# A joint image-text attention block: the image probabilities are transposed by ScalarE's DMA queue instead of TensorE

## The chip, the cores and the metric

The kernel runs on one core of one Trainium2 chip. The metric is the time of one execution in microseconds of device time, as a median of several runs. The engines are named as in the profile: PE is TensorE (PEld its weight loads), DVE is VectorE, ACT is ScalarE, POOL is GpSimd, SP is SyncE. A name with a q behind it (SPq, ACTq) is that engine issuing a DMA.

## The reference

Two streams, image (2 batches of 256 tokens) and text (2 batches of 32 tokens), each 1152 wide, in bfloat16. Each stream is layer-normed and modulated by rows computed from `c`; the two are joined for one softmax attention of 288 tokens per batch, projected back separately, gated and added to the input.

```python
hi = _layernorm(x_img) * (1 + sci) + shi          # 2 x 256 x 1152
ht = _layernorm(x_txt) * (1 + sct) + sht          # 2 x 32 x 1152
qkvi, qkvt = hi @ wqkv_img, ht @ wqkv_txt
q, k, v = concat of text and image parts          # 2 x 288 x 1152
p = softmax(q @ k^T * D ** -0.5)                  # 2 x 288 x 288
a = p @ v
out_i = x_img + gai * (a[:, 32:] @ wo_img)
out_t = x_txt + gat * (a[:, :32] @ wo_txt)
```

## The kernel before

The order of the work on every engine is the order in which the kernel's text issues it (`manual_schedule`); waits between engines are put in by the framework. Eleven weight matrices of 2.65 MB (1152 x 1152) stream in on SP's queue in the order of their use, through a ring of five buffers and two fixed homes. The stages on PE, one after another: the modulation scale and the image values (`v_wide`, L255), the image queries and keys (`qk_img`, L512), rows of the text modulation (L402, L406), the text queries and keys (`qk_txt`, L580), then the stage that the change is in, then the output projection (`out_chunk`, L845).

The stage of the change, in its order before:

1. `scores_img` (L613): for each of four blocks (batch b, block q of 128 query tokens) PE computes 128 x 288 scores by nine products; DVE takes the row maximum (L597), ACT the exponential with its row sum (L600, tile `e`), DVE the reciprocal and the scaled probabilities `pb` (L604, L605: 128 x 288, bfloat16), and POOL copies the text columns of `pb` into `px` (L607).
2. `scores_txt_and_gate`: PE makes the text scores (L626, both batches in one tile of 64 rows) and rows of the image gate (L630, L635). ACT copies a first piece of the gate rows to SBUF (L638, `g_sb`), and POOL stores it to a scratch in DRAM by two DMAs (L640). Then comes `softmax_txt` (ACT L669) and the next gate piece (ACT L642). PE makes the text values (L688) and the rest of gate and values (L646, L651, L654). `softmax_txt_norm` gives `pb_tt` (DVE L675), whose text columns POOL copies into `px_t` (L676). The end of the stage takes the text values (DVE L657), the last gate piece (ACT L658, POOL L660) and the last block of values (ACT L661) out.
3. `p_transposes`: for each half kj of the 256 image keys, PE transposes the five 128 x 128 blocks (four image, one text) into one PSUM tile `pk` (L697, ten products against the identity), and DVE (kj = 0) or ACT (kj = 1) copies each batch's 288 columns to `pTs[b]` (L704). Three more transposes make `pX` from the `px` tiles (L707), for the products against the text values.
4. `attn_out`: sums of the values by the transposed probabilities, in three groups of output blocks (L753), with DVE and ACT taking the results out (L766, L768). `full_ops` gives the order inside a group: kj outside, batch inside, so that the first eight products need both batches' first halves.

Behind it POOL reads the gate rows back from DRAM, broadcast over 128 partitions (L803, `gb`), and multiplies a third of the output weights by them (L829, `w_og`); DVE multiplies and adds each output chunk (L851, L852).

A DMA signals its end on one of eight semaphores in rotation, and a DMA that takes a semaphore again waits for the DMA that had it before.

Of the kernel before, what the change touches and what calls it, by code (L numbers as in the profile page):

```python
# [14 lines left out]
def kernel(  # L15
# [14 lines left out]
    nc = tc.nc  # L30
    bf = mybir.dt.bfloat16
    f32 = mybir.dt.float32
    PSUM = bass.MemoryType.PSUM

    B, NI, D = x_img.shape
    NT = x_txt.shape[1]
    P = 128
    KT = D // P
    NTOK = NI + NT
    NIT = (B * NI) // P  # L40
    TPB = NI // P
    NTT = B * NT
    CH = 384
    NCH = D // CH
    VC = 288
# [12 lines left out]
    ps_mm = ctx.enter_context(tc.tile_pool(name="ps_mm", bufs=7, space=PSUM))  # L58
# [11 lines left out]
    def w_view(src):  # L70
        return src.rearrange("(kt p) n -> p kt n", p=P)

    def load_w(src, c0, ksplits=((0, KT),), home=None):
        t = wpool.tile([P, KT, D], bf, tag="w", name="t") if home is None else act.tile([P, KT, D], bf, tag=home, name="w_home")
        for (k0, k1) in ksplits:
            nc.sync.dma_start(t[:, k0:k1, :], w_view(src)[:, k0:k1, c0:c0 + D])
        return t
# [35 lines left out]
    K3 = ((0, 3), (3, 6), (6, KT))  # L113
    K2 = ((0, 5), (5, KT))
# [4 lines left out]
    ident = const.tile([P, P], bf)  # L119
# [64 lines left out]
    v_t = act.tile([P, VW], bf)  # L184
    v_t8 = act.tile([NTT, P], bf)
# [193 lines left out]
    pbs = {}  # L379
# [3 lines left out]
    pxs = [act.tile([P, 2, B, NT], bf, name=f"px_{q}") for q in range(TPB)] + [act.tile([P, 2, B, NT], bf, name="px_t")]  # L383
# [38 lines left out]
    def cols_out(dst, cps, add):  # L422
        nc.vector.tensor_scalar_add(dst, cps[:].rearrange("p (k b) -> p k b", b=B), add)
# [14 lines left out]
    v_wide_out(3, 1)  # L438
    evac(v_i[:, :, NM:D], vacc["n"][:])

    w_k_i = load_w(wqkv_img, D, K3)
    w_sh_t = load_w(wmod_txt, 0)
    w_sc_t = load_w(wmod_txt, D, K2)
    nc.sync.dma_start(x_t[0:P:P // NTT, :], xt_flat[:, :])
    w_q_t = load_w(wqkv_txt, 0, K2)
    w_k_t = load_w(wqkv_txt, D, K2)
    w_ga_i = load_w(wmod_img, 2 * D, K2, home="V")
    w_v_t = load_w(wqkv_txt, 2 * D, K3)
# [4 lines left out]
    gsc = tc.dram_tile([B, D], bf, name="mod_scratch")  # L453
# [136 lines left out]
    qk_txt(w_k_t, 1)  # L590


    qpos = [[0, P, 2 * P], [NT, NT + P, 0]]

    def softmax_img(sps, key):
        nmx = small.tile([P, 1], f32, tag="nmx")
# [6 lines left out]
    def softmax_norm(key, e, rs):  # L603
        nc.vector.reciprocal(rs[:], rs[:])  # L604
        nc.vector.tensor_scalar_mul(pbs[key][:], e[:], rs[:])  # L605
        b, q = key
        nc.gpsimd.tensor_copy(pxs[q][:, :, b, :], pbs[key][:, NI:NTOK].unsqueeze(1).to_broadcast([P, 2, NT]))  # L607

    def scores_img(b, qi):
        q0 = qi * P  # L610
        sps = ps_mm.tile([P, NTOK], f32, tag="mm")
        for ft in range(KT):
            nc.tensor.matmul(sps[:], lhsT=qkTs[0][:, ft, b, q0:q0 + P], rhs=qkTs[1][:, ft, b, :],  # L613
                             start=(ft == 0), stop=(ft == KT - 1))
        return softmax_img(sps, (b, qi))

    CW = 544
    GW = VC + P
    GR = (D - 2 * GW) // NGG

    def scores_txt_and_gate():
        sps = ps_mm.tile([P, NTOK], f32, tag="mm")
        gps = ps_mm.tile([P, GW + GR], f32, tag="mm")
        for ft in range(KT):
            for b in range(B):
                nc.tensor.matmul(sps[NT * b:NT * (b + 1), :], lhsT=qkTs[0][:, ft, b, NI:NTOK], rhs=qkTs[1][:, ft, b, :],  # L626
                                 start=(ft == 0), stop=(ft == KT - 1), tile_position=(0, NT * b))
            for g in range(2):
                r = 64 + 32 * g
                nc.tensor.matmul(gps[r:r + 32, 0:VC], lhsT=sT32[:, ft, :], rhs=w_ga_i[:, ft, g * GW:g * GW + VC],  # L630
                                 start=(ft == 0), stop=(ft == KT - 1), tile_position=(0, r))
        for kt in range(KT):
            for g in range(NGG):
                c0 = 2 * GW + g * GR
                nc.tensor.matmul(gps[32 * g:32 * g + 32, GW:GW + GR], lhsT=sT32[:, kt, :], rhs=w_ga_i[:, kt, c0:c0 + GR],  # L635
                                 start=(kt == 0), stop=(kt == KT - 1), tile_position=(0, 32 * g))
        g_sb = work.tile([P, CW], bf, tag="garow2", bufs=1)
        nc.scalar.copy(g_sb[:, GW:GW + GR], gps[:, GW:GW + GR])  # L638
        for b in range(B):
            nc.gpsimd.dma_start(gsc[b, 2 * GW:D].rearrange("(g j) -> g j", g=NGG), g_sb[b:P:32, GW:GW + GR])  # L640
        st = softmax_txt(sps)
        nc.scalar.copy(g_sb[64:P, 0:VC], gps[64:P, 0:VC])  # L642
        vps = v_txt_wide()
        for kt in range(KT):
            for b in range(B):
                nc.tensor.matmul(gps[NT * b:NT * (b + 1), VC:GW], lhsT=hT_t[:, kt, NT * b:NT * (b + 1)],  # L646
                                 rhs=w_v_t[:, kt, NM:D], start=(kt == 0), stop=False,
                                 tile_position=(0, NT * b))
            for g in range(2):
                r = 64 + 32 * g  # L650
                nc.tensor.matmul(gps[r:r + 32, VC:GW], lhsT=sT32[:, kt, :], rhs=w_ga_i[:, kt, g * GW + VC:(g + 1) * GW],  # L651
                                 start=(kt == 0), stop=(kt == KT - 1), tile_position=(0, r))
        for b in range(B):
            nc.tensor.matmul(gps[NT * b:NT * (b + 1), VC:GW], lhsT=selS[:, b, :], rhs=svn[:],  # L654
                             start=False, stop=True, tile_position=(0, NT * b))
        softmax_txt_norm(*st)
        nc.vector.tensor_sub(v_t[:], vps[:], v_t[:])  # L657
        nc.scalar.copy(g_sb[64:P, VC:GW], gps[64:P, VC:GW])  # L658
        for b in range(B):
            nc.gpsimd.dma_start(gsc[b, 0:2 * GW].rearrange("(g j) -> g j", g=2), g_sb[64 + b:P:32, 0:GW])  # L660
        nc.scalar.copy(v_t8[:], gps[0:NTT, VC:GW])  # L661

    def softmax_txt(sps):
        q = NTT
        nmx = small.tile([P, 1], f32, tag="nmx")
        nc.vector.reduce_max(nmx[0:q, :], sps[0:q, :], axis=AX.X, negate=True)
        e = work.tile([P, NTOK], f32, tag="of", bufs=1, name="e")
        rs = small.tile([P, 1], f32, tag="rst", bufs=1)
        nc.scalar.activation(e[0:q, :], sps[0:q, :], ACT.Exp, bias=nmx[0:q, :], scale=1.0, accum_out=rs[0:q, :])  # L669
        return e, rs  # L670
# [8 lines left out]
    pTs = [work.tile([P, 2, NTOK], bf, tag="pT", name=f"pT{b}") for b in range(B)]  # L679
# [10 lines left out]
                                     start=(kt == 0), stop=(kt == KT - 1), tile_position=(0, r))  # L690
        return ps

    def p_transposes():
        pt = pbs["t"]
        def wide(pk, kj, srcs):
            for src, q0 in srcs:
                nc.tensor.transpose(pk[:, q0:q0 + P], src[:, kj * P:(kj + 1) * P], ident[:])  # L697

        for kj in range(TPB):
            pk = ps_mm.tile([P, B * NTOK], bf, tag="mm", name="pk")  # L700
            wide(pk, kj, [(pbs[(0, 0)], 0), (pbs[(0, 1)], P), (pt, NI),
                          (pbs[(1, 0)], NTOK + NT), (pbs[(1, 1)], NTOK + NT + P)])
            for b in range(B):
                (nc.scalar.copy if kj else nc.vector.tensor_copy)(pTs[b][:, kj, :], pk[:, b * NTOK:(b + 1) * NTOK])  # L704
        pX_ps = ps_mm.tile([P, 2 * NT + NI], bf, tag="mm", name="pX_ps")
        for px, x0 in ((pxs[TPB], 0), (pxs[0], 2 * NT), (pxs[1], 2 * NT + P)):
            nc.tensor.transpose(pX_ps[:, x0:x0 + P], px[:].rearrange("p g b t -> p (g b t)"), ident[:])  # L707
        svp = ps_sm.tile([P, NCOL + B], f32, tag="sm", name="svp")
        select_cols(strips["svr"], svp)
        nc.vector.tensor_copy(pX[:, 0:NTOK], pX_ps[:, NT:NT + NTOK])  # L710
        nc.vector.tensor_copy(pX[:, NTOK:NTOK + NT], pX_ps[:, 0:NT])
        cols_out(sv, svp, 0.0)
# [16 lines left out]
        return {(dt, b): [(acc_bank(), 0, 0, NTOK)] for dts_ in dts for b in range(B) for dt in dts_}  # L729

    def full_ops(dts, acc):
        return [(dt, b, kj, pc) for kj in range(TPB) for b in range(B) for dt in dts for pc in acc[dt, b]]

    def text_ops(dts, acc):
        return [[(dt, b, None, acc[dt, b][n]) for b in range(B)] for dt in dts for n in range(len(acc[dt, B - 1]))]
# [37 lines left out]
    def attn_out():  # L773
# [15 lines left out]
        run(fC + flat(tC), fC + flat(tC))  # L789
        acc_evac(accC, [(dt, b) for b in range(B) for dt in GC])  # L790

    s00 = scores_img(0, 0)
    s01 = scores_img(0, 1)
    softmax_norm(*s00)
    s10 = scores_img(1, 0)
    softmax_norm(*s01)
    s11 = scores_img(1, 1)
    softmax_norm(*s10)
    softmax_norm(*s11)
    scores_txt_and_gate()  # L800
    gb = act.tile([P, B, D], bf, tag="Bt")
    for b in range(B):
        nc.gpsimd.dma_start(gb[:, b, :], gsc[b, :].partition_broadcast(P))  # L803
    xt_q = xt_flat.rearrange("(q h) (g j) -> g q h j", h=2, g=NGG)
    for g in range(NGG):
        nc.gpsimd.dma_start(xf[32 * g:32 * g + 32, :, :], xt_q[g])
    p_transposes()
    aT = act.tile([P, KT, B * NTOK], bf, tag="Q")
    attn_out()

# [112 lines left out]
```

## Time and profile before

| | |
|---|---|
| median of 3 runs | 114.87 us (114.75 to 115.28) |
| the profiled execution | 115.62 us, of which its span 113.8 us |
| PE busy | 109.1 us, 96% of the span |
| DVE, ACT, POOL busy | 76.0, 37.4, 27.6 us |
| SP's DMA queue | 39.05 MB, 89.8% of the 16 DMA engines' span |
| ACT's DMA queue | 0.77 MB, 2.2% |
| TensorE clock granted | 0.998 |

The chain of waits follows the work that ended last back to its start. A line of it gives start, length and what; `x10` means ten instructions. In the timeline a line gives start, busy time, engine, line, operation, `out<-in` with shapes, and in brackets the idle time before it with what ended it. A DMA issue line gives what is moved, from which queue, how often, the size of one and the median time from issue to landing.

### The profile page before, as it was taken

The page shows a single profiled execution, that of the slowest core. Times are in us where ns is not written, and L with a number is a line of the kernel's source. Part 1 is how long each engine was busy: PE and PEld are TensorE (multiplying, and loading weights), DVE is VectorE, ACT ScalarE, POOL GpSimd, SP SyncE. Part 2 cuts the span into 40 slices and gives each one's busy share as a digit, 9 for nine tenths or more (in the row PEclk, how much of TensorE's full clock was granted, in tenths as well). Part 3 has the DMA queues.
Part 4 walks back from the last instruction along what each step waited for, and adds up shares of the span by engine and source line. Part 5 has one row for each costly group of instructions (what it writes and reads, how often), then busy time and mean ns, then how long its engine had stood idle before and what let it go on. Part 6 is the DMA issues. An engine that isn't in the chain of part 4 may idle for free.

```text
span 113.8 us, 2918 instructions
## 1 busy us (share of the span) xinstructions
PE 109.1 (96%) x1227; PEld 65.0 (57%) x1227; DVE 76.0 (67%) x151; ACT 37.4 (33%) x86; POOL 27.6 (24%) x60
## 2 busy tenths in 40 slices
PE   5999997999999999999999999999999999999990
PEld 1356663655644444444446659787687565667670
DVE  1699330756299999999999860236666802998771
ACT  4627500272290062640008934015546700001000
POOL 7000120640050000000000050601450460699300
PEclk9999999999999999999999999999999999999999
DMA  3999999999999999999999999999999999983052
GB/s 84 327 352 344 375 374 408 410 410 413 405 411 407 411 413 405 410 411 412 412 409 412 413 403 406 407 396 377 407 411 404 409 412 407 378 328 132 12 178 69
DMA packets 22839, 40.87 MB, mean 359 GB/s; under 512 B 1375, under 2 KB 6635, under 8 KB 22827
## 3 DMA queue, kind: packets, MB, share of 16 engines
q1 hardware_dynamic: 21547, 39.05, 89.8%
q10 hardware_dynamic: 672, 0.77, 2.2%
q0 software_dynamic: 608, 0.88, 2.1%
q8 instruction: 9, 0.15, 0.5%
q14 instruction: 3, 0.02, 0.1%
HBM read 39.36 MB, written 1.34 MB: 358 GB/s over the span
## 4 chain that ended last, share of the span: by engine, by line
PE 80%; SPq 8%; DMA 8%; issue 1%; DVE 0%
PE qkps L512 31%; PE ps L845 16%; DMA w_sc_i<-in_wmod_img_dram 8%; PE va L255 7%; SPq L98 6%; PE aps L753 5%; PE ps L580 4%; PE sps L613 4%; PE gps L402 3%; PE ops L863 2%; PE ps L688 2%; SPq L94 1%; PE van L267 1%; PE gps L818 1%; PE sps L626 1%; PE mps L217 1%
## 5 line engine op out<-in xcount | busy, mean ns | idle before, releaser
L512 PE MATMUL qkps<-hT_i,t 128*128 128x512 bf16 x162 | 35.6, 379 | 0.0
L512 PEld LDWEIGHTS <-t 128*128 128x128 bf16 x162 | 15.6, 98 | 18.6 <-issue 0.2
L474 DVE SCALAR_TENSOR_TENSOR sacc<-w_v_i,mod_img,sacc 128x1152 f32<-128x1152 bf16 x16 | 22.7, 1419 | 0.5
L255 PE MATMUL va<-w_v_i,hT_i 128*128 128x512 bf16 x72 | 17.5, 380 | 0.0
L845 PE MATMUL ps<-t,aT 128*128 128x384 bf16 x99 | 16.4, 326 | 0.0
L845 PEld LDWEIGHTS <-aT 128*128 128x128 bf16 x117 | 11.0, 98 | 6.9 <-issue 0.5
L851 DVE TENSOR_TENSOR tmp<-ps,gb 128x384 bf16<-128x384 f32 x11 | 6.1, 550 | 6.1 <-DMA gb<-mod_scratch 5.0
L829 POOL TENSOR_TENSOR w_og<-t,gb 128x384 bf16<-128x384 bf16 x9 | 8.7, 1004 | 4.6 <-DMA gb<-mod_scratch 4.6
L255 PEld LDWEIGHTS <-hT_i 128*128 128x128 bf16 x72 | 6.3, 98 | 5.6 <-ACT hT_i L201 0.4
L533 POOL TENSOR_SCALAR svn<-svr 128x128 bf16<-128x128 bf16 x1 | 0.3, 299 | 33.0 <-ACT svr L154 33.0
L140 PE MATMUL wps<-wz 128*128 128x512 bf16 x15 | 6.5, 613 | 1.2 <-DVE wz L125 1.2
L166 DVE BATCH_NORM_STATS2 stats<-x_i 128x6 f32<-128x384 bf16 x12 | 5.8, 541 | 2.5 <-DMA x_i<-in_x_img_dram 2.5
L462 ACT ACTIVATE qT<-qkps 128x512 bf16<-128x512 f32 x9 | 4.7, 602 | 7.1 <-PE qkps L512 7.1
L478 ACT CAST shi<-sacc 128x1152 bf16<-128x1152 f32 x2 | 2.3, 1152 | 13.0 <-DVE sacc L474 13.0
L240 POOL TENSOR_SCALAR hT_i<-hT_i,mod_img 128x128 bf16<-128x128 bf16 (+1 forms) x5 | 2.1, 435 | 15.8 <-DVE mod_img L225 15.8
L766 DVE TENSOR_SCALAR aT<-aps,sv 128x288 bf16<-128x288 f32 (+2 forms) x11 | 4.3, 456 | 2.0 <-PE aps L753 2.0
L235 DVE TENSOR_SCALAR hT_i<-hT_i,mod_img 128x256 bf16<-128x256 bf16 (+1 forms) x16 | 4.3, 328 | 1.7 <-ACT hT_i L212 1.5
L580 PEld LDWEIGHTS <-t 128*128 128x128 bf16 x162 | 5.0, 98 | 0.5
L154 DVE CAST kT<-qkps 128x512 bf16<-128x512 f32 x3 | 2.1, 686 | 4.7 <-PE qkps L512 4.7
L580 PE MATMUL ps<-hT_t,t 128*128 128x64 bf16 x162 | 5.1, 193 | 0.0
L852 DVE TENSOR_TENSOR o<-tmp,x_i 128x384 bf16<-128x384 bf16 x11 | 4.7, 426 | 0.4
L753 PE MATMUL aps<-pT,v_i 128*128 128x288 bf16 (+2 forms) x44 | 4.8, 265 | 0.0
(167 smaller groups left out, 146.2 us busy)
## 6 DMA issues: line engine op xcount, KB each, us to landing
t<-in_wqkv_img_dram SPq DMA_DIRECT2D x6, 864.0 KB, 13.0
t<-in_wmod_txt_dram SPq DMA_DIRECT2D x2, 2592.0 KB, 17.6
t<-in_wqkv_txt_dram SPq DMA_DIRECT2D x2, 1440.0 KB, 14.2
t<-in_wmod_img_dram SPq DMA_DIRECT2D x3, 864.0 KB, 12.3
t<-in_wqkv_txt_dram SPq DMA_DIRECT2D x3, 864.0 KB, 14.2
t<-in_wo_txt_dram SPq DMA_DIRECT2D x3, 864.0 KB, 15.5
t<-in_wqkv_txt_dram SPq DMA_DIRECT2D x2, 1152.0 KB, 15.0
w_v_i<-in_wqkv_img_dram SPq DMA_DIRECT2D x7, 288.0 KB, 7.1
```

Of the source, the lines that this page charges most:

```text
L98: nc.sync.dma_start(w_v_i[:, kt:kt + 1, :], w_view(wqkv_img)[:, kt:kt + 1, 2 * D:3 * D])
L140: nc.tensor.matmul(ps[:], lhsT=wz[:, 0:P], rhs=wz[:], start=True, stop=True)
L166: nc.vector.bn_stats(stats[0:np_, k, :], x_ap[:, k * CH:(k + 1) * CH])
L255: nc.tensor.matmul(ps[:], lhsT=hT_i[:, kt, i * P:(i + 1) * P], rhs=w_v_i[:, kt, half * VW:(half + 1) * VW], start=(kt == 0), stop=(kt == K ...
L462: nc.scalar.mul(out_ap, in_ap, SCALE)
L474: nc.vector.scalar_tensor_tensor(saccs[b][:], w_v_i[:, kt, :], ap, saccs[b][:], op0=ALU.mult, op1=ALU.add)
L512: nc.tensor.matmul(pss[j - j0][:], lhsT=wq[:, kt, j * P:(j + 1) * P], rhs=hT_i[:, kt, :], start=(kt == 0), stop=(kt == KT - 1))
L580: nc.tensor.matmul(ps[:, j - j0, :], lhsT=wq[:, kt, j * P:(j + 1) * P], rhs=hT_t[:, kt, :], start=(kt == 0), stop=(kt == KT - 1))
L753: nc.tensor.matmul(bank[:, off:off + c1 - c0], lhsT=lhsT, rhs=rhs, start=(first[id(bank)] == n), stop=(final[id(bank)] == n))
L829: nc.gpsimd.tensor_mul(w_og[:, dt, 0:CH], w_o_i[:, dt, NG0:D], gb[:, B - 1, NG0:D])
L845: nc.tensor.matmul(ps[:, 0:cw], lhsT=aT[:, dt, t0:t0 + P], rhs=rhs, start=(dt == DTS[0]), stop=(dt == DTS[-1]))
L851: nc.vector.tensor_mul(tmp[:, 0:cw], ps[:, 0:cw], gb[:, b, cs])
```

## The change

The image probabilities no longer pass through PE. As soon as a block `pb` is normalised, ACT issues one transposing DMA of its 128 x 256 image columns straight into `pTs[b]` (four in all, `p_transposed`). Text's probabilities are transposed by two products with a right side of 64 columns instead of 128, whose result DVE (batch 0) and ACT (batch 1) copy; the three `pX` transposes become products into a float32 tile. `full_ops` sums batch by batch instead of half by half. In `scores_txt_and_gate` the text softmax is issued ahead of the first gate piece, and the last outputs (`values_out`) go behind the text transposes. Three weight loads that were split into 3, 2 and 2 DMAs are one DMA each, so that SP issues four fewer.

```diff
-    w_k_i = load_w(wqkv_img, D, K3)
+    w_k_i = load_w(wqkv_img, D)
...
-    w_sc_t = load_w(wmod_txt, D, K2)
+    w_sc_t = load_w(wmod_txt, D)
...
-    w_q_t = load_w(wqkv_txt, 0, K2)
+    w_q_t = load_w(wqkv_txt, 0)
...
+        st = softmax_txt(sps)
         g_sb = work.tile([P, CW], bf, tag="garow2", bufs=1)
         nc.scalar.copy(g_sb[:, GW:GW + GR], gps[:, GW:GW + GR])
         for b in range(B):
             nc.gpsimd.dma_start(gsc[b, 2 * GW:D].rearrange("(g j) -> g j", g=NGG), g_sb[b:P:32, GW:GW + GR])
-        st = softmax_txt(sps)
...
-        nc.vector.tensor_sub(v_t[:], vps[:], v_t[:])
-        nc.scalar.copy(g_sb[64:P, VC:GW], gps[64:P, VC:GW])
-        for b in range(B):
-            nc.gpsimd.dma_start(gsc[b, 0:2 * GW].rearrange("(g j) -> g j", g=2), g_sb[64 + b:P:32, 0:GW])
-        nc.scalar.copy(v_t8[:], gps[0:NTT, VC:GW])
+        def values_out():
...
+        return values_out
...
-    def p_transposes():
+    def p_transposes(values_out):
         pt = pbs["t"]
-        for kj in range(TPB):
-            pk = ps_mm.tile([P, B * NTOK], bf, tag="mm", name="pk")
-            wide(pk, kj, [(pbs[(0, 0)], 0), (pbs[(0, 1)], P), (pt, NI),
-                          (pbs[(1, 0)], NTOK + NT), (pbs[(1, 1)], NTOK + NT + P)])
-            for b in range(B):
-                (nc.scalar.copy if kj else nc.vector.tensor_copy)(pTs[b][:, kj, :], pk[:, b * NTOK:(b + 1) * NTOK])
-        pX_ps = ps_mm.tile([P, 2 * NT + NI], bf, tag="mm", name="pX_ps")
-        for px, x0 in ((pxs[TPB], 0), (pxs[0], 2 * NT), (pxs[1], 2 * NT + P)):
-            nc.tensor.transpose(pX_ps[:, x0:x0 + P], px[:].rearrange("p g b t -> p (g b t)"), ident[:])
+        pk = ps_mm.tile([P, TPB, NTT], f32, tag="mm", name="pk")
+        for kj in range(TPB):
+            nc.tensor.matmul(pk[:, kj, :], lhsT=pt[:, kj * P:(kj + 1) * P], rhs=ident[:, 0:NTT], start=True, stop=True)
+        for b in range(B):
+            (nc.scalar.copy if b else nc.vector.tensor_copy)(
+                pTs[b][:, :, qpos_t[b]:qpos_t[b] + NT], pk[:, :, NT * b:NT * (b + 1)])
+        values_out()
+        pX_ps = ps_mm.tile([P, NTT + NI], f32, tag="mm", name="pX_ps")
+        for px, x0, n in ((pxs[TPB], 0, NTT), (pxs[0], NTT, P), (pxs[1], NTT + P, P)):
+            nc.tensor.matmul(pX_ps[:, x0:x0 + n], lhsT=px[:].rearrange("p g b t -> p (g b t)"), rhs=ident[:, 0:n],
+                             start=True, stop=True)
...
-        return [(dt, b, kj, pc) for kj in range(TPB) for b in range(B) for dt in dts for pc in acc[dt, b]]
+        return [(dt, b, kj, pc) for b in range(B) for kj in range(TPB) for dt in dts for pc in acc[dt, b]]
...
+    def p_transposed(b, q):
+        q0 = qpos[b][q]
+        nc.scalar.dma_start_transpose(pTs[b][:, :, q0:q0 + P], pbs[(b, q)][:, 0:NI])
+
     s00 = scores_img(0, 0)
     s01 = scores_img(0, 1)
     softmax_norm(*s00)
+    p_transposed(0, 0)
     s10 = scores_img(1, 0)
     softmax_norm(*s01)
+    p_transposed(0, 1)
     s11 = scores_img(1, 1)
     softmax_norm(*s10)
+    p_transposed(1, 0)
     softmax_norm(*s11)
-    scores_txt_and_gate()
+    p_transposed(1, 1)
+    values_out = scores_txt_and_gate()
+    p_transposes(values_out)
...
-    p_transposes()
```

## The prediction, made before the changed kernel ran

> **What bounds the kernel now.** I read the page's busy times first, then the chain of waits in order of time around the transposes, then the timeline of that stretch by engine, then the DMA issues.
>
> ```profile
> PE 109.1 (96%) x1227; PEld 65.0 (57%) x1227; DVE 76.0 (67%) x151; ACT 37.4 (33%) x86; POOL 27.6 (24%) x60
> ...
> 83.50 0.67 PE pk L697 x10
> 84.17 0.17 PE pX_ps L707 x3
> 84.33 0.03 PE svp L418 x2
> 84.37 0.02 PE svp L420
> 84.39 5.43 PE aps L753 x66
> ```
>
> The first line is the page's; the rest is the chain. From 31.93 to 111 us the chain holds PE and nothing else, so PE time saved in this stage is saved whole, and a wait put on PE is paid whole. All the transposes cost PE 0.84 us. That is the ceiling of the gain.
>
> ```profile
> 78.96 0.50 ACT L600 ACTIVATE e<-sps,nmx 128x288 f32<-128x288 f32 x1 [0.57 <-DVE rs L604]
> 80.06 0.50 ACT L600 ACTIVATE e<-sps,nmx 128x288 f32<-128x288 f32 x1 [0.51 <-DVE rs L604]
> 80.88 0.37 DVE L605 TENSOR_SCALAR pb<-e,rs 128x288 bf16<-128x288 f32 x1
> 81.06 0.23 ACT L638 CAST g_sb<-gps 128x80 bf16<-128x80 f32 x1 [0.41 <-PE gps L635]
> 81.58 1.16 POOL L640 DMA_DIRECT2D mod_scratch<-g_sb  x2
> 81.65 0.49 ACT L669 ACTIVATE e<-sps,nmx 64x288 f32<-64x288 f32 x1 [0.36 <-DVE nmx L666]
> 82.05 0.19 ACT L669 ACTIVATION_READ_ACCUMULATOR e<-sps,nmx 64x1 f32 x1
> 82.92 0.29 POOL L676 COPY px_t<-pb_tt 128x128 bf16<-128x128 bf16 x1 [0.18 <-DVE pb_tt L675]
> ```
>
> The timeline gives the dates that matter. The last block of image probabilities is ready at 81.25 us, only 2.2 us ahead of its transpose at 83.5. ACT's gaps between the exponentials are 0.5 us each. POOL's two stores end 0.2 us before `px_t` is made, which PE needs at 84.17.
>
> ```profile
> v_t<-shift_scratch POOLq DMA_DIRECT2D x4, 32.0 KB, 5.4
> out_dram<-o ACTq DMA_DIRECT2D x1, 64.0 KB, 1.6
> mod_scratch<-g_sb POOLq DMA_DIRECT2D x2, 0.6 KB, 5.2
> gb<-mod_scratch POOLq DMA_DIRECT2D x2, 288.0 KB, 6.7
> x_i<-in_x_img_dram ACTq DMA_DIRECT2D x2, 288.0 KB, 3.2
> ```
>
> The last column is us from issue to landing. The small transfers that POOL issues between 66 and 91 us, while SP's weight stream fills the 16 engines (397 to 409 GB/s), take 4.5 to 6.7 us. ACT's own 64 KB store at the end, with the stream over, takes 1.6, and its loads at the start 3.2.
>
> **The change, part by part.**
>
> *PE's saving.* Of ten `pk` transposes (0.67 us, 0.067 each) eight go and two stay with 64 columns; L580's 81 products of 64 columns take 2.36 us in the chain, 0.029 each, so 0.06 us: 0.61 saved. One `pX` product narrows by the same 0.03. Total 0.64 us. But the first sum now waits for DVE's copy of text's columns: the second product ends some 0.19 us after its start (L580's mean), near 83.75, and a copy of 32 columns (L711) took 0.17. So the sums could start near 84.0 instead of 84.39: 0.4 us at most.
>
> *The transposing transfers, T1 to T4.* No transpose by DMA is in the trace. Two costs are unknown, and I bound both. The issue holds ACT: its DMA issues of 36 to 288 KB took 0.36 to 0.65 us; SP's under the stream took up to 3.9 (`w_o_i`), but SP's queue is full of its own loads and ACT's is empty, so I take 0.65. The landing: from 1.6 (ACT, no stream) to 6.7 (`gb`, with stream). I take 5.2, the row in the middle of POOL's, because the stream runs. By 0.65 ACT's order comes out so: T1 from 78.40 (behind the second exponential) to 79.05; third exponential, 0.59 with its sum, to 79.64; T2 to 80.29; fourth exponential to 80.88; T3 to 81.53; the last `pb` is ready 0.60 later, 81.48, as before (80.65 to 81.25); T4 from 81.53. It lands at 81.53 + 5.2 = 86.7. T2 lands at 84.8.
>
> *The wait on PE.* Summing batch by batch puts T3 and T4 behind the first eight products, 0.8 us. Before, the second eight started at 84.39 + 0.8 = 85.2. Now they start at 86.7: **+1.5 us**. Everything on PE behind them moves with it.
>
> *The gate piece behind the text softmax.* The exponential of text starts when T4 is issued, 82.18 instead of 81.65, and ends at 82.77. Only then ACT copies the gate piece (0.23, to 83.00); before, this copy ran at 81.06, ahead of it. POOL's two stores start 0.29 later, as before (81.29 to 81.58), and take 1.16: 83.29 to 84.45. The copy of `px_t` is queued behind them on POOL: 84.5 to 84.8. PE's `pX` products wait for it, and ahead of the sums in PE's order: sums from 84.8 + 0.14 + 0.06 = 85.0, 0.6 later than before. With the shortest issue (0.36) ACT is not late, and the same sum gives 84.5, 0.1 later. So the saving is gone even where the transfers are free. In the forecast this wait is hidden under T4's.
>
> *Edits with nothing to pay.* The merged loads need the whole matrix at once: the last piece of `w_k_i` was issued at 28.5 and landed 13 us later, 41.5, and the keys start at 49.4; `w_sc_t` landed by 37.86 + 16.9 = 54.8, needed at 62.3; `w_q_t` by 46.55 + 15.0 = 61.6, needed at 68.4. SP's first two `w_o_t` pieces now wait for T1 and T2 (their semaphores); SP has `w_ga_t` queued ahead, 2592 KB issued at 76.16 behind `w_o_i`, so the stream does not run dry, and `w_o_t` is used at 102.8. The last third of `w_v_t` landed at 67.93 + 13.7 = 81.6 and is used near 82.3; T1 to T3 bring 192 KB, 0.5 us at 400 GB/s, so it may be just late; that stall ends before T4 lands. The last gate piece leaves ACT some 1.1 us later (behind the text columns' copy), and so `gb` comes later; DVE had idled 5 us for `gb` with PE four chunks ahead of seven buffers, and PE itself is 1.5 late, so nothing.
>
> *The sum.* 115.62 + 1.5 = 117.1 for a profiled execution (span 115.3); the median lies 0.75 under that execution, so 114.87 + 1.5 = **116.4 us**.
>
> **A rule against the change.** In the chain a transpose on PE costs 0.067 us; nothing here shows one by DMA. The Trainium skill, VectorE: DVE Perf Modes, in "The three transpose paths", gives 390 ns for 128 x 128 in bfloat16 on TensorE against 1309 ns by the DMA crossbar, and advises TensorE where PSUM will do as the target. By it the eight blocks, one behind another from 78.4, would end at 88.9, an estimate of +3.7 and 118.6 us; no run here shows that yet.
>
> **The rivals.**
>
> *The transfers are hidden.* If T4 lands within 4.0 us of its issue, the wait for it is gone, and `px_t` decides: +0.1 to +0.7, 115.0 to 115.6. For it: ACT's own rows of 1.6 to 3.2. Against: none of those had the stream beside it. This one ends at no change. A gain would need ACT to issue faster than any row shows.
>
> *ACT is held at the issue.* If ACT's issues are held as SP's are, 2 us each, T4 starts at 85.6 and lands at 90.8: +5.6, 120.5 us. From 0.7 us per issue on, each further 0.1 costs about 0.3. For it: SP's issues of 2.0 to 3.9 us under the stream. Against: those are long because SP's own queue is full.
>
> *The transfers run one behind another.* If T2 does not start before T1 has ended, and each takes the 3.2 us of ACT's loads, T4 ends at 78.4 + 12.8 = 91.2: +6.0, 120.9 us. It decides from 2 us each on. For it: they share a queue, and small pieces interleave with the stream's. Against: SP's queue has several loads in flight. The skill's figures above are this case at a lower price.
>
> **How the numbers follow.** T4 late by the rows: 0.50, from 4.5 us (+0.8) to 6.7 (+3.0), 115.7 to 117.9. Hidden: 0.28, of which 0.20 within 0.5% (0.57 us, about what a measurement of this kernel can tell from no change), 0.05 slower and 0.03 faster. Held at the issue: 0.10. One behind another: 0.12. Slower is 0.50 + 0.05 + 0.10 + 0.12 = 0.77. The range goes from 114.7, a little under the hidden case, to 120.2, which leaves out the upper halves of the last two (0.11) and most of what is faster.
>
> **What would show it.** In the profile after: `pk` x2 near 0.06 us in the chain; an idle stretch of PE at the ninth sum of 128 x 288, ended by a DMA into `pT`; landings of the transposes near 5 us; ACT issues near 0.65; `px_t` on POOL right behind two stores and near 84.5. If PE waits for POOL's `px_t` and for no DMA, the first rival is right. If PE already waits long at the first sum, it is one of the other two: ACT's issue lengths tell which. I am wrong throughout if PE shows no wait between 83 and 88 us.

## The result, and the profile after

| | before | after |
|---|---|---|
| median | 115.08 us (4 runs, 114.75 to 115.35) | 124.2 us (4 runs, 123.93 to 124.55) |
| ratio | | 1.0796 (95% interval 1.0753 to 1.0840) |
| span of the profiled execution | 113.8 us | 122.8 us |
| granted clock, mean | 0.998 | 0.958 |

The kernel became slower by 8%, about 9.1 us. The prediction had the direction (slower, 116.4 us) but neither the time nor the range (up to 120.2 us). Two of the profiles further down, that with the filler and that of the rest of the change, were taken in executions 1.5 and 2.3% longer than the fastest of their kernel, so only lengths inside the stage are read from them.

From the page of the profile after, PE's busy time and the clock granted to it in 40 slices of the span (3.07 us each):

```profile
PE 110.9 (90%) x1219; PEld 65.5 (53%) x1219; DVE 77.3 (63%) x150; ACT 37.0 (30%) x85; POOL 27.2 (22%) x60
PEclk9999999999999999999999999999555799999999
```

PE has eight instructions fewer and is 1.8 us busier. The digits 555 say why: for three slices it ran at about half its clock. That stretch begins inside the stage of the change. To size it I cut both executions at the first text score (L626 before, L627 after) and at the first product of the output projection. The columns are the window with its length, the busy time of PE, PEld, DVE, ACT and POOL, then the granted clock, the DMA share and GB/s. First before, then after:

```profile
79.40:89.75 10.35, 10.35 (x230) 7.80 (x229) 6.86 (x23) 5.92 (x20) 3.24 (x8) 1.00 1.04 408
89.75:113.80 24.05, 21.27 (x227) 13.78 (x225) 14.66 (x31) 1.68 (x4) 12.02 (x15) 0.99 0.66 249
```

```profile
78.84:98.74 19.90, 13.30 (x221) 8.64 (x221) 7.01 (x22) 5.99 (x19) 6.57 (x14) 0.74 1.08 366
98.74:122.80 24.06, 21.27 (x227) 13.78 (x225) 15.71 (x31) 1.68 (x4) 8.32 (x9) 1.00 0.37 135
```

The whole loss is in this stage: 19.90 us instead of 10.35. The output projection takes 24.05 and 24.06. Before, PE was busy in all of the 10.35 us. After, it idles 6.60 of 19.90 us, and its work takes 13.30 instead of the 9.71 that the prediction's saving of 0.64 would leave: 3.59 us more, put down here to the lower clock. So 10.35 - 0.64 + 6.60 + 3.59 = 19.90. The 3.59 is what is left over in this sum and no measurement; the run with the filler below checks it.

The waits of PE in that stage, from the list of waits after (total us, times, longest):

```profile
PE aps L756 <- DMA pT<-pb: 3.6, 2, 2.1
PE gps L647 <- ACT g_sb L643: 2.5, 1, 2.5
PE pX_ps L709 <- POOL px_t L681: 0.5, 1, 0.5
```

The first line is two waits, 1.54 us for T2 at the first sum and 2.08 us for T4 at the ninth. The second line was in no term of the prediction. ACT's timeline after shows where it comes from:

```profile
77.71 1.90 ACTq L797 DMA_TRANSPOSE pT<-pb  x1
79.72 0.50 ACT L601 ACTIVATE e<-sps,nmx 128x288 f32<-128x288 f32 x1 [1.89 <-DVE nmx L598]
79.83 1.18 ACTq L797 DMA_TRANSPOSE pT<-pb  x1
81.11 0.50 ACT L601 ACTIVATE e<-sps,nmx 128x288 f32<-128x288 f32 x1 [0.80 <-DVE pb L606]
81.22 1.19 ACTq L797 DMA_TRANSPOSE pT<-pb  x1
82.50 1.21 ACTq L797 DMA_TRANSPOSE pT<-pb  x1
83.76 0.50 ACT L674 ACTIVATE e<-sps,nmx 64x288 f32<-64x288 f32 x1 [2.05 <-issue]
84.48 0.39 ACT L643 CAST g_sb<-gps 64x288 bf16<-64x288 f32 x1
```

The second column of an ACTq line is the time for which the issue holds ACT: 1.18 to 1.90 us. The label on the idle time of the third exponential (79.72) names DVE, but the issue above it had ACT until 79.61. Text's exponential starts at 83.76, against 81.65 before, and the gate piece of L643 behind it, whose source PE wants to overwrite, ends at 84.87: PE had reached that point at 82.40.

The chain of waits after, from the last block's probabilities to the output:

```profile
81.94 0.37 DVE pb L606
82.31 0.20 DVE nmx L671
82.50 9.37 DMA pT<-pb
91.87 0.14 issue
92.00 6.81 PE aps L756 x58
98.81 11.81 PE ps L856 x72
```

A DMA now carries the chain through the stage: T4, 9.37 us from issue to landing. The four landed in 6.8, 8.4, 8.9 and 9.4 us; the view of the tile `pT` gives the shortest, the median and the longest:

```profile
DMA to landing us min/median/max: 6.8/8.6/9.4
```

The 58 products behind T4 took 6.8 us; the last 58 of the 66 had 4.55 before (89.75 - 85.2).

### The profile page after: what moved, and what is told of

It is laid out like the page before. It is cut to its first block, busy times and chain, and to the rows that moved or that the text cites. A ratio compares the mean times of both kernels' runs of the same rounds, so it can differ in the third digit from the quotient of the medians.

```text
span 122.8 us, 2906 instructions
## 1 busy us (share of the span) xinstructions
PE 110.9 (90%) x1219; PEld 65.5 (53%) x1219; DVE 77.3 (63%) x150; ACT 37.0 (30%) x85; POOL 27.2 (22%) x60
## 5 line engine op out<-in xcount | busy, mean ns | idle before, releaser
L756 PE MATMUL aps<-pT,v_i 128*128 128x288 bf16 (+2 forms) x44 | 7.3, 339 | 3.6 <-DMA pT<-pb 3.6
L756 PEld LDWEIGHTS <-v_i 128*128 128x128 bf16 x44 | 4.7, 123 | 5.9 <-issue 4.2
L771 ACT ACTIVATE aT<-aps,sv 128x288 bf16<-128x288 f32 (+2 forms) x11 | 4.3, 456 | 9.0 <-PE aps L756 8.8
L863 DVE TENSOR_TENSOR o<-tmp,x_i 128x384 bf16<-128x384 bf16 x11 | 6.2, 568 | 0.4
L140 PE MATMUL wps<-wz 128*128 128x512 bf16 x15 | 4.9, 486 | 1.2 <-DVE wz L125 1.2
```

The costliest lines, as they stand in the source:

```text
L140: nc.tensor.matmul(ps[:], lhsT=wz[:, 0:P], rhs=wz[:], start=True, stop=True)
L756: nc.tensor.matmul(bank[:, off:off + c1 - c0], lhsT=lhsT, rhs=rhs, start=(first[id(bank)] == n), stop=(final[id(bank)] == n))
L863: nc.vector.tensor_add(o[:, cs], tmp[:, 0:cw], x_i[:, i, cs])
```

## The experiments

Theory A after this result: the transfers land late because of the weight stream beside them, and hold ACT because a transposing issue is long; the half clock follows from PE's idling. Rivals: the transposing itself is what is slow to land; the hold comes from the full queues, or goes with the size; the rest of the change (edits other than the transfers) costs time by itself; the slower products are a cost of the new layout, not of the clock.

**No stream beside the transfers.** The four weight loads that stream during the stage are left out, and a matrix that is already there stands in for each, so the results differ.

```diff
-    w_v_t = load_w(wqkv_txt, 2 * D, K3)
+    w_v_t = w_k_t
...
-    w_o_i = load_w(wo_img, 0, K2)
+    w_o_i = w_k_t
...
-    w_ga_t = load_w(wmod_txt, 2 * D)
+    w_ga_t = w_k_t
...
-    w_o_t = load_w(wo_txt, 0, K3)
+    w_o_t = w_k_t
```

> The changed kernel without the weight stream beside the transposes: the text values, both output projections and the text gate use the text keys' matrix, so four loads (10.6 MB) are left out and the results differ. In the changed kernel the four transposes landed 6.8 to 9.4 us after their issue and held ACT 1.2 to 1.9 us each. Theory A (the stream makes the landing long): without it they land within 3.2 us, the last near 85.5 us; PE then waits only for ACT's late gate piece, some 2.5 us, the clock stays at 1.0, profiled time about 118. Theory B (a transposing transfer is that slow by itself): landings stay at 7 to 9 us, PE waits as in the changed kernel, time about 124 to 125. The issue length tells by itself: still 1.2 us if it is the instruction's own, about 0.4 if it was the stream's pressure.

Measured: 119.25 us (one run), before 114.91 beside it. The DMA issues and PE's waits of this run:

```profile
pT<-pb ACTq DMA_TRANSPOSE x4, 3.0
```

```profile
PE gps L647 <- ACT g_sb L643: 2.5, 1, 2.5
PE pX_ps L709 <- POOL px_t L681: 0.4, 1, 0.4
```

The landings fall to 2.4 to 3.3 us and PE's waits for `pT` are gone: the stream makes the landings late. The issues stay at 1.18 to 1.82 us with the queues empty, and so does the wait of 2.5 us behind them. The hold therefore belongs to the instruction, not to the stream. The clock did not stay at 1.0 as expected: 0.54 was granted from 86.60 to 89.54 us, the first sixteen sums took 2.95 us, and the time is 1.25 us above the expected 118. The stage took 14.54 us.

**Plain copies in place of the transposes**: the same bytes, copied in pieces of 256 bytes. The transposition is left out, so the sums take other numbers.

```diff
-        nc.scalar.dma_start_transpose(pTs[b][:, :, q0:q0 + P], pbs[(b, q)][:, 0:NI])
+        nc.scalar.dma_start(pTs[b][:, :, q0:q0 + P], pbs[(b, q)][:, 0:NI].rearrange("p (k j) -> p k j", k=2))
```

> The changed kernel with the four transposes replaced by plain copies of the same bytes in the same 256-byte runs from ACT's queue; the transposition is left out, so the sums take untransposed probabilities. Theory A (any small transfer from this queue is that late under the stream): copies land 7 to 9 us after issue and the time stays near 124. Theory B (transposing costs it): copies land in 4.5 to 6.7 us like POOL's small ones, ACT's issue takes 0.4 to 0.65, the last lands near 87, PE waits about 1.5 us in all, time about 116 to 117.5.

Measured: 123.18 us (one run), stage 18.64. Issues and waits:

```profile
pT<-pb ACTq DMA_DIRECT2D x4, 64.0 KB, 8.5
```

```profile
PE aps L756 <- DMA pT<-pb: 5.4, 2, 2.9
PE gps L647 <- ACT g_sb L643: 0.2, 1, 0.2
```

A copy lands as late as a transpose (median 8.5 against 8.6 us). The Trainium skill, Advanced Engine Details and Errata, in "X-Bar Transpose (TRN2)", has transposing DMAs as fast as regular ones; for the landing these rows agree. They do not for the issue: a copy held ACT 0.60 to 0.72 us, a transpose 1.18 to 1.90. With the copies the gate piece is nearly on time, but PE waited longer for the landings instead (5.4 us, not 3.6), and the stage is only 1.26 us shorter. Under late landings most of the hold is hidden.

**Fewer packets for the same bytes.** Plain copies again, each partition's 512 bytes in one run; the transposition is left out here too. The tiles are cleared ahead of them on POOL.

```diff
+        nc.scalar.dma_start(pTs[b][:].rearrange("p k n -> p (k n)")[:, q * NI:(q + 1) * NI], pbs[(b, q)][:, 0:NI])
```

> As the plain copies before, but each of the four copies goes out in runs of 512 bytes instead of 256: the same bytes in half as many packets (128 instead of 256 each; the order inside a tile is not the reference's). Theory (under the stream a packet of ACT's queue takes turns with the stream's, so that this queue drained 158 packets per us in the plain-copy run, and the four transfers' 1,088 packets took 6.9 us): the packets take half as long in all, about 3.5 us, the landing falls from 8.5 to 5 to 6.5 us, the last lands near 86.5, and the time falls from 123.2 to 116 to 118. Rival (a fixed delay of the loaded queue of 8 us, or one by bytes): landing stays near 8.5 and the time near 123.

Measured: 120.25 us (one run), stage 15.59. The landings came as expected, 5.5 to 7.1 us; the time did not: it is 2.25 us above the upper end. PE still waited twice ahead of the sums:

```profile
PE aps L758 <- ACT pT L706: 2.6, 1, 2.6
PE aps L758 <- DVE pT L706: 0.6, 1, 0.6
```

The names are those of the copies of text's columns. In this layout a transfer writes over the place of these columns, so the copies stand behind the landings too (ACT waited 5.5 us there, DVE 2.0), and PE behind the copies. The clock also fell (0.89 over the stage), which the expectation had left out.

ACT's queue carried 672 packets before, 1760 with the 256-byte copies (272 per transfer) and 1248 with the 512-byte ones (144). With 128 packets fewer each and the same bytes, the median landing is 2.3 us shorter. That would be some 18 ns a packet, but the median holds the wait behind the transfers ahead in the same queue. The first transfer, with none ahead of it, landed only 0.8 us sooner (5.5 instead of 6.3 us), the last 2.6 us (7.1 instead of 9.7). So under the stream packets cost, above all those of the transfers ahead; of the first one's landing some 4.6 us do not go with its packets (an estimate from the two first transfers). The Trainium skill, DMA: Bandwidth & Descriptors, in "Queues, rings and completion order", says that an engine serves the queues that have work in turn, one packet at a time. That would let a queue of small packets move at the pace of the stream's larger ones. The rows do not speak against it, but the section counts several descriptors to a packet, so its packets need not be those that the profile counts, and no run here shows the turns themselves.

**PE kept busy while it waits**: products against a tile of zeros, in three places, into a tile that nobody reads.

```diff
         vps = v_txt_wide()
+        fill(10)
...
-        run(fA, fA + flat(tA))
+        half = len(fA) // 2
+        fill(6)
+        run(fA[:half], fA + flat(tA))
+        fill(9)
+        run(fA[half:], fA + flat(tA))
...
+    def fill(n):
+        ps = ps_mm.tile([P, VW], f32, tag="mm", name="fps")
+        for _ in range(n):
+            nc.tensor.matmul(ps[:], lhsT=wz[:, 0:P], rhs=wz[:], start=True, stop=True)
```

> The changed kernel with 25 idle products of 128 x 512 on PE put into its three waits (10 ahead of the rest of gate and values, 6 ahead of the first sums, 9 between the batches). Theory (the half clock is what PE's idling brings, and costs 2.9 us of the 9.1): the granted clock stays 1.0 in this stage, the sums take 5.4 to 6 us where they took 8.3, the landings stay, and the time falls by 2 to 3 us to about 121.5 to 122.2. Rival (the sums are slow because the transfers and the stream load their operands' memory): the clock in the rows or the sums' length does not change, time 124 or a little more.

Measured: 122.1 us, ratio 1.0599 (1.0556 to 1.0643) against 1.0796 without the filler, so 2.0% of the time before, some 2.3 us, came back; the stage took 17.45 us instead of 19.90. PE's timeline with the filler, then that of the change as it was; the second column is the time of the products in the line:

```profile
92.85 0.90 PE L757 MATMUL aps<-pT,v_i 128*128 128x288 bf16 x8 [1.04 <-DMA pT<-pb]
94.16 3.12 PE L757 MATMUL aps<-pT,v_i 128*128 128x288 bf16 x28
```

```profile
92.00 1.60 PE L756 MATMUL aps<-pT,v_i 128*128 128x288 bf16 x8 [2.08 <-DMA pT<-pb]
94.37 4.09 PE L756 MATMUL aps<-pT,v_i 128*128 128x288 bf16 x28
```

The same eight products take 0.90 instead of 1.60 us, and the granted clock is 1.0 from 86 to 96 us. The landings are as late as in the change (6.7 to 9.3 us). The layout is not at fault; idling is. Without the filler's 5.82 us PE was busy 10.08 us of this stage, against 13.30 in the change: the slower clock cost some 3.2 us by this count (an estimate). Work that nobody needs made the changed kernel faster. The Trainium skill, TensorE: Matmul & The Clock Gate, in "HAM oscillation — how this bites in real kernels", describes this: waits for data let the array's clock drop to half, and the work behind them starts slow. The trace agrees: 0.5 was granted in the window from 88.0 to 92.0 us and 0.67 in that from 92.0 to 98.7. The Trainium skill and the trace differ in the length: the section's rule is about gaps of more than some 3.4 us, and no wait of PE in this stage was longer than 2.53.

**The rest of the change alone**: the four image blocks go over PE as before, by eight transposes into PSUM tiles of their own that DVE and ACT copy out; everything else stays changed.

> The rest of the change alone: merged loads, the text softmax ahead of the gate piece, text by half-width products, sums batch by batch, but the image blocks transposed on PE as before and no transfer on ACT's queue. Theory (all the loss is the transfers': landing, issue and the clock that PE's waits bring): 114.6 to 115.4, ratio 0.995 to 1.003. Rival (the text softmax's new place or the merged loads carry a part): 116 or more, with PE waiting for the gate piece or for px_t.

Measured: 115.77 us, ratio 1.0059 (1.0036 to 1.0082); stage 10.65 us. The stage is 0.30 us longer than before. In the chain of this run DVE's copies out of PSUM, that of text's columns last, stand between the transposes and the first sum. The merged loads, the order of the sums, the text products and the moved gate piece together cost 0.6%, not 8%.

**The same with the gate piece ahead of the text softmax again**:

```diff
-        st = softmax_txt(sps)
         g_sb = work.tile([P, CW], bf, tag="garow2", bufs=1)
...
+        st = softmax_txt(sps)
         nc.scalar.copy(g_sb[64:P, 0:VC], gps[64:P, 0:VC])
```

> The rest of the change alone (no transfers) with one part of it undone: ACT copies the first gate piece ahead of the text softmax again. The rest alone came out at 1.0059 of before (1.0036 to 1.0082), with PE 0.44 us idle for px_t behind POOL's two stores and the gate rows later. Theory (that place carries it): PE's wait for px_t is gone, ratio 0.996 to 1.001, 114.4 to 115.0 us. Rival (the smaller PSUM copies, the order batch by batch or the merged loads carry it): ratio stays at 1.004 to 1.008.

Measured: 115.38 us, ratio 1.0037 (1.0017 to 1.0057). The stage took 10.60 us, against 10.65. The theory fell. The wait of 0.44 us for `px_t` that the expectation names is not among PE's waits in that run; it is one of the changed kernel (0.45). In both traces the chain to the first sum goes through DVE's copy of text's columns, and the list names it here with 0.23 us. The intervals of the two runs overlap, so a gain from this edit is not settled; it did not bring back the whole 0.6%.

**Four transposing transfers that nobody reads**, on top of the rest alone: same places, same 128 x 256, into a spare tile.

```diff
+    spare = act.tile([P, 2 * D], bf, tag="sacc", name="spare")
...
+        n, c0 = 2, NI * (TPB * b + q)
+        nc.scalar.dma_start_transpose(spare[:, c0:c0 + n * P].rearrange("p (k j) -> p k j", k=n), pbs[(b, q)][:, 0:256])
```

> The rest of the change alone plus the four transposing transfers into a spare tile that nobody reads: the image blocks come from PE. It has ACT's hold and the traffic without anybody waiting for a landing. Theory (ACT is held 1.2 to 1.9 us per issue, the text softmax and the gate pieces leave ACT 2.1 us late, PE waits 2.5 us for them and then runs part of the sums at half clock): 118 to 119.7, PE waits 2.3 to 2.6 us for the gate piece. Rival (only the landing costs): 115.5 to 116.3.

Measured: 118.13 us, ratio 1.0255 (1.0223 to 1.0286), against 1.0059 without them. The waits and the issues:

```profile
PE gps L647 <- ACT g_sb L643: 2.3, 1, 2.3
```

```profile
spare<-pb ACTq DMA_TRANSPOSE x4, 8.3
```

Nobody waits for these landings, and still the kernel loses 2.0%: ACT was held 1.57, 1.20, 1.18 and 1.21 us, the gate piece came late, and in the profiled execution the first sixteen sums took 2.85 us (1.64 in the rest alone). There the single wait of 2.25 us, over at 84.84, was enough to bring the granted clock to 0.5 from 85.8 to 89.2 us. It did not always: the mean granted clock was 0.985 in the executions of 118.51 and 119.23 us, but 0.998 and 1.000 in those of 117.60 and 117.74. So the loss is in part the wait and in part, in half of the executions, the clock.

**The same with half the size** (128 x 128 each):

> The same with spare transposes of half the width (128 x 128 each, 8 tiles of 16 x 128 instead of 16). Theory (the issue's length goes with the tiles): 0.6 to 0.85 us per issue, PE waits for the gate piece below 1 us, time 116 to 117. Rival (a fixed length per transposing issue): 1.1 to 1.2 us, time as with the full ones.

Measured: 119.53 us (one run; 116 to 117 was expected, and the full transfers took 117.60 to 119.23); issues of 1.55, 1.11, 1.11 and 1.20 us, PE's wait 2.05 us, median landing 7.0 instead of 8.3 us. Half the tile saved under 0.1 us of each issue. The theory that the hold goes with the tiles fell: it is close to a fixed price per transposing issue. The landing fell with the packets (160 instead of 288 each), but the bytes are halved too. Beside the 512-byte copies it shows that bytes are not what counts: these had twice the bytes in 144 packets and landed in 6.2 us.

**One unread transfer instead of four** (the first):

> The rest of the change alone, with one transposing transfer (image block 0, 0) into a spare tile nobody reads; the image blocks go over TensorE as before. Theory: four such transfers cost 2.5 us because each holds ACT 1.2 to 1.6 us (together 5.2 us with the first), and the gate piece behind them is late. With one, ACT is held some 1.6 us, nearly all of it where ACT would have waited anyway: TensorE's wait for the gate piece is under 0.6 us, the stage is 10.6 to 11.3 us, the time 115.3 to 116.8. The transfer lands 6 to 7 us after its issue: its own 288 packets and the late start under the stream, and nothing queued behind it. Rival: the first transposing transfer of the kernel costs something of its own (a stall of ACT, or of the stream) whatever follows: then the time stays above 117 us.

Measured: 116.29 us (one run), stage 11.14, PE's wait for the gate piece 0.3 us. The issue took 1.59 us and the landing 7.2, a little above the expected 7. One hold fits nearly into the time for which ACT waits anyway; four in a row don't. That first transfer had nothing ahead of it in ACT's queue, so most of the late landing is there without any queueing among the four.

**The four unread transfers after the sums:**

```diff
     attn_out()
+    for b in range(B):
+        for q in range(TPB):
+            p_transposed(b, q)
```

> The rest of the change alone, with the four transposing transfers into a spare tile nobody reads, issued by ACT after attn_out's copies instead of inside the softmax stage. Theory: the unread transfers cost time only through what ACT has queued behind them; here that is the output stage's evictions, which have slack. Time 115.3 to 116.8, ratio 1.003 to 1.015, stage 10.6 us, granted clock near 1.0 throughout; issues 1.1 to 1.6 us each as before, landings 6 to 10 us while the stream runs and 2.4 to 3.5 us once it is over. Rival: the transfers cost by their traffic or by their kind wherever they stand (stream slowed, output weights late): then 117 us or more, with TensorE waiting for the output weights in the output stage.

Measured: 116.31 us, ratio 1.0120 (1.0082 to 1.0158); stage 10.72, clock 1.0, landings 8.8 to 10.3 us, the longest above the expected 10. The spare tile in this run:

```profile
L808 ACTq DMA_TRANSPOSE spare<-pb x4: 1260/1271/1637, 90.3 to 94.6; - x4
DMA to landing us min/median/max: 8.8/8.9/10.3
```

The three numbers in the first line are the shortest, median and longest issue in ns. The same four instructions with the same holds cost 1.4% less here than inside the softmax stage: most of what they cost is what ACT has queued behind them. Some 0.6% above the rest alone remains, with no wait in the profile to match. Where it is stays open; the two intervals touch (1.0082), so its size is not settled, and that the traffic itself costs this much is not ruled out.

## Why the prediction was right or wrong

- **The landing** was the term that broke the sum: "I take 5.2, the row in the middle of POOL's", with 6.7 as the upper bound. T4 took 9.37 us. The rows it was taken from were those of another queue with fewer packets: POOL's sixteen transfers had 608 together. Under the stream a landing grows with packets (8.5 against 6.2 us for the same bytes), and each of these had 288, with up to three others ahead of it. The upper bound, `gb`, came from POOL's queue as well.
- **The hold**: "SP's queue is full of its own loads and ACT's is empty, so I take 0.65." A plain copy from ACT's queue did take 0.60 to 0.72. A transposing issue takes 1.1 to 1.9 us, with or without the stream, at half size too. The rival "ACT is held at the issue" had the mechanism, at a wrong reason (a full queue) and 2 us each. T4 was issued at 82.50, not 81.53. PE also waited 1.54 us at the first sum, which the prediction had named as a sign of this rival or the next.
- **With these two terms** the prediction's own sum gives +1.5 + 0.97 + 4.17 = +6.6 us. The slower clock adds 2.2 for the 58 products behind T4 (6.74 - 4.55): +8.8, 123.7 us, near the 124.2 measured. So the wait was put in the right place and the ninth sum was the right point; its size was off by 5.1 us.
- **The clock** was in no term. The prediction treated a wait as idle time alone. Here the work behind the wait slowed as well, and 2.3 us came back when PE was kept busy. So a wait was paid more than whole.
- **Who waits behind ACT**: the prediction followed the gate piece to `px_t` (0.45 us, as it came: PE waited from 85.83 to 86.28 for a copy that ended at 86.22) but not the next gate piece, L643, whose source PE needs empty. That wait was 2.5 us, the first in the stage. In the change it lies beside T4's flight, so it adds little there; where nobody waits for the landings, it and the clock behind it are most of the 2.3 us that the unread transfers cost.
- **One behind another** was priced at 120.9 us for 3.2 us each. T1 alone already took 6.8, so the queue among the four adds at most 2.6 us to T4; the stream is the larger part.
- **A rule against the change**: the figure of the Trainium skill, VectorE: DVE Perf Modes, in "The three transpose paths", for a transpose by DMA (118.6 us by it) had the right sign and was nearer than the forecast, but short too. Without the stream the landings of two blocks each, 2.4 to 3.3 us, are close to two of its 1309 ns; with it they are 6.8 to 9.4.
- **Right**: a wait of PE at the ninth sum decides; the eight transposes that go are worth little (0.46 us in the run of the rest alone, where they are back; the prediction has 0.54 for them); the merged loads and SP's longer waits cost nothing that can be seen (from the image queries to the first text score 47.44 against 47.47 us, output projection 24.06 against 24.05); and no gain came of the change.

No version that was run beats the kernel before. The nearest, the rest of the change with the gate piece put back, stands at 1.0037.

## What to carry to other kernels

A small transfer that is needed soon should not be sent through DMA engines that a weight stream fills: price it by a row of the same queue, with as many packets and under the same load, and compare that with the time it is away from its use. An issue that holds an engine costs what that engine has queued behind it, so follow every instruction behind it, not only the one on the known path. And where PE will idle for a microsecond or two, add to the wait the slower clock of the work behind it.

## What the runs showed of the hardware that was not expected

- A transposing issue on ACT's queue held ACT 1.11 to 1.90 us, a plain one of the same 64 KB 0.47 to 0.72; size (128 x 128 or 128 x 256) and the stream made little difference.
- While the weight stream ran at about 400 GB/s, 64 KB in 256-byte pieces took 6.3 to 10.3 us to land, transposed or not; in 512-byte pieces 5.5 to 7.1; transposed with the stream away 2.4 to 3.3.
- In six traces the granted clock fell to 0.5 between 0.7 and 1.5 us behind the end of a wait of PE of 2.05 to 2.90 us: in the changed kernel, without the stream, with both kinds of copies and with the unread transfers, full and half. One such wait sufficed, though not in every execution. The half clock lasted 3.4 us in four of the traces, 6.8 with the 256-byte copies and 10.2 in the changed kernel, where more waits followed. Eight sums took 1.60 us instead of 0.90.
- With four transposing transfers in the softmax stage, the stream itself nearly stopped for a while: 10 GB/s from 85.5 to 86.5 us in the changed kernel, and gaps like it in the runs with the filler and with the unread transfers. Beside the plain copies no quarter of a microsecond from 82 to 91 us fell under 349 GB/s. The copies landed as late, so this gap does not explain the landings; what causes it stays open.
